# Talking-heads attention and a squared-ReLU feed-forward on one core: the score copies of a batch's last 64 tokens, one QK tile in batch 0, an earlier guard branch, and a new order of TensorE's work

## The chip, the cores and the metric

The kernel runs on one NeuronCore of a Trainium2 chip, as one program. The core has five engines that run side by side: TensorE (PE, matrix products; PEld is its weight load), VectorE (DVE), ScalarE (ACT), GpSimd (POOL) and SyncE (SP), and 16 DMA engines that all issue queues share. The metric is the device time of one execution in microseconds (us), the median of several. Matrix products write to PSUM, which has eight banks here; ACT or VectorE copy ("evict") each result to SBUF before its bank can be used again.

## The reference

Eight batches, twelve heads, 448 tokens, 64 channels per head; then a feed-forward over 8 x 448 = 3584 tokens of 768 channels.

```
scores = scale * q @ k.transpose(0, 1, 3, 2)
scores = einsum('bhij,hg->bgij', scores, w_pre)       # heads mixed before the softmax
attn   = exp(scores - max);  attn = attn / (sum(attn) + 1e-09)
attn   = einsum('bhij,hg->bgij', attn, w_post)        # heads mixed after the softmax
x      = (attn @ v), tokens x (heads * channels)
out    = (max(x @ w_in, 0) ** 2) @ w_out              # 768 -> 2048 -> 768
```

## The kernel before

**Stages of a batch.** Tokens are taken in chunks of ten (`CH`), 45 chunks per batch, the last one in two halves of four. A chunk holds 10 tokens x 12 heads = 120 rows, so that mixing the heads becomes a product with a 120-wide block matrix. A batch goes through these units on TensorE, each named in the code:

- `tr`: transposes of q and k (lines 833 and 837), copied to `qkt`.
- `qk`: scores of a tile of 128 tokens for one pair of heads (lines 975 and 985). The result, 128 tokens x 448 keys per head, is copied to `stage` (`sev`). The last tile of batches 1 to 7 has 64 tokens; there one unit does two pairs of heads, one in the upper and one in the lower 64 partitions of the bank, and each half is copied by itself: 64 partitions, twelve copies per batch.
- `rel`: a transfer on SP's queue that carries a chunk from `stage` (tokens in partitions) to `dring` (token and head in partitions); line 1030. `dring` has 16 slots, so a slot is written again when the pre unit 16 chunks earlier is done.
- `pre`: heads mixed before the softmax, two chunks at a time (lines 1054, 1061, 1069), followed by `exp` on ACT (line 1094), which also sums the rows.
- `rec` and `fold`: the reciprocal of the row sums and its product with the second mixing matrix, on POOL (lines 1117 and 1127; on VectorE for the first ten chunks).
- `post`: heads mixed after the softmax, transposed on the way (line 1159), copied to `a2t`.
- `av`: the product with v (lines 1216 and 1237), copied to `xt`.
- `h` and `o`: the two feed-forward products (lines 1288 and 1296; 1375, 1427 and 1435), with relu and square between them on ACT and VectorE; results go from `osb` to DRAM on SP's queue, the last ones on ACT's too.

In batch 0 the first 30 chunks (`ND`) don't go through `stage`: their scores are computed from a spread copy of q straight in dring's layout (`spr`, line 916). The remaining 148 tokens are two QK tiles (`NQ0`), each computed 128 tokens wide.

**Forms of a unit.** Many units can run as full 128-row products, as two row tiles of 64, or as four 64 x 64 quarters. The form is written into the order.

**What sets the order.** TensorE's order is the string `ORDER`: each character names the stream from which the next unit is taken and its form. A planner (`_Plan`) walks through it with a price for each task and places all other work: an eviction goes to whichever of ACT and VectorE would end it first by its prices, and the other engines' tasks are placed in the order in which they become ready. Every engine then executes its list in order, with semaphore waits. The price of `rec` on POOL is 120 ns (line 1123), while a `rel` is held at 1000 ns on SP.

**The guard.** The fast program takes the softmax without subtracting the maximum. VectorE checks the row sums once the last exp is done (`good0` to `good2`), SP turns the result into one row (`turn`), VectorE reduces it to one flag. At its end each engine waits for the flag, loads it (line 1631) and branches (line 1632): past a slow program with the maximum, in the normal case. SP's very last task, `final`, the waits for all outputs (line 1574), stands inside the branch.

Of the kernel before, what the change touches and what calls it, by code (L numbers as in the profile page):

```python
# [12 lines left out]
ACT = "act"  # L13
DVE = "dve"
POOL = "pool"
SP = "sp"
# [13 lines left out]
ORDER = (  # L30
    "0000511100551155555555555555555c2155555035bcb02515525353c2c5155c1531333355c2555c355332c0"
    "240443c4b200gh1111h62b3g33hqc31cgc3h2b3hgh3bbbch3633r3gb42444223g1h72qgqb2733g1r12q713h3"
    "6b2673722392003t122j33t2b282bi338333s04202444bb002gqbb28311i313s111s322gh2227hqh3613q1hr"
    "3363q2422444br2br631q1731h613q32h0220gh22qg373r3c38212i3s333814144420022ghh20028118111i1"
    "33s339b22j31t22193229119313t3319242444312q2bq227373163c3631731h2020q1g2br2h236333q20b0r2"
    "r20038318311i33184bb42244229c19311t133t118222833i313s242444232q2b623713733631g12r2br2006"
    "33q33rb17q200262r217293c3t331t2200jc181118133s311842244422391319313t13392422444222838333"
    "i311i31qb2b62qb2622h73733373q1b6rb00h2q0202q22h700239331911j11193182238318331s2424442228"
    "1s311i333814244413bq22g2rb2r23631q32r2br23633g31r002h2633q733r024044412tb2j0209bb2t23811"
    "381138333s11t22jb2922t23831s33i1318b4244422bq2bqb27337631q33731r2q21q2r22h1633673373bs22"  # L40
    "842i2i244422383833s333s22qr6r22293933t33tq4q444hghh6gq7g6hrghisrggh7hg7giqishhjjijtsttsj"
    "j"
)
# [329 lines left out]
def bass_talking_heads_attention__then__ffn_squared_relu_kernel(  # L373
# [17 lines left out]
    IT = 128  # L391
    ND = 30
    NE = 6
    NQ0 = 2
    QT0 = tuple((CH * (ND + x * (NCH - ND) // NQ0),
# [20 lines left out]
    with ExitStack() as es:  # L416
# [76 lines left out]
        def program(guard):  # L493
# [461 lines left out]
            def emit_QK(b, T):  # L955
# [7 lines left out]
                i0 = min(ta, S - w)  # L963
                for p in ((0, 3, 1, 4, 2, 5) if n == 0 else range(0, NP, IT // w)):
                    g = _Group(2)

                    quad = w == PJ
                    f = None if quad else _Flex(False)

                    def fn_qk(eng, en, p=p, g=g, f=f):  # L970
                        r_ = None
                        if f is not None and f.alt:
                            for x, y in QUADS:
                                r0 = 64 * x
                                r_ = eng.matmul(  # L975
                                    ps[y * PJ:(y + 1) * PJ, g.banks[x], 0:S],
                                    qkt[r0:r0 + 64, pb, p, 0, i0 + y * PJ:i0 + (y + 1) * PJ],
                                    qkt[r0:r0 + 64, pb, p, 1, :],
                                    start=True, stop=True,
                                )  # L980
                            return r_
                        for x, y in QUADS:
                            if y * w < IT:
                                r0 = 64 * x
                                r_ = eng.matmul(  # L985
                                    ps[y * w:(y + 1) * w, g.banks[x], 0:S],
                                    qkt[r0:r0 + 64, pb, p + y, 0, i0:i0 + w],
                                    qkt[r0:r0 + 64, pb, p + y, 1, :],
                                    start=True, stop=True,
                                )  # L990
                        return r_

                    t_qk = unit(s_QK, "qk%d_%d_%d" % (b, T, p), fn_qk,
                                [trev[(b, p + y)] for y in range(IT // w)]
                                + [trev.get((b, p + y, 0)) for y in range(IT // w)],
                                190.0, "quad" if quad else "row", g,
                                4 if quad else 2, f, [("quad", 190.0, 4)])
                    t_qk.after += old
                    for x, y in QUADS:
                        if y * w >= IT:  # L1000
                            continue

                        def fn_sev(eng, en, x=x, y=y, p=p, g=g):
                            return copy(eng, en, stage[0:w, sl, head(p + y, x), :],
                                        ps[w * y:w * y + w, g.banks[x], 0:S])

                        t_sev = add("sev%d_%d_%d_%d" % (b, T, p + y, x), FLEX, fn_sev, [t_qk] + old,
                                    c_ev(S), b * 1000.0 + 20 + 10 * T)
                        g.readers[x].append(t_sev)
                        sev_of[n].append(t_sev)  # L1010
# [3 lines left out]
                for c in range(NCP):  # L1014
                    i, nv = c * CH, CH
                    if c >= NCH - 1:
                        nv = TAIL // 2
                        i = S - TAIL + (c - NCH + 1) * nv
                    a, e = max(i, ta), min(i + nv, tb)
                    if a < e:  # L1020
                        emit_rel(b, c, n, a - i0, a - i, e - a)

            def emit_rel(b, c, n, r0, d0, nv):
                g = b * NCP + c
# [3 lines left out]
                def fn(eng, en):  # L1028
                    o = R0 + d0 * H
                    eng.dma_start(dring[o:o + nv * H, slot, :],  # L1030
                                  stage[r0:r0 + nv, n % 2, :, :]).then_inc(sem.handle, 16)

                t = plan.add("rel%d_%d_%d" % (b, c, d0), SP, fn, sev_of[n],
                             {SP: (1000.0, 0.0)}, g * 1.0, sem, 16,
                             dma=("move", 10.0 + 73.3 * nv, 54.0))
# [50 lines left out]
            def after_pre(g, t_pre, gr, x):  # L1086
# [28 lines left out]
                def fn_rec(eng, en):  # L1115
                    if en == POOL:
# [419 lines left out]
            if not guard:  # L1536
# [87 lines left out]
        def emit_engine(eng_name, eng):  # L1624
            tasks = fast[eng_name]
            k = len(tasks)
            while k and tasks[k - 1].name == "final":
                k -= 1
            emit_tasks(eng_name, eng, tasks[:k], fast_waits)
            eng.wait_ge(t_flag.sem.handle, t_flag.semval)  # L1630
            fine = eng.value_load(flag[0:1, 0:1])
            with eng.If(fine == 0):
# [56 lines left out]
```

## Time and profile before

| | |
|---|---|
| median of the runs | 533.03 us (531.01 to 534.14) |
| the profiled execution's own time | 531.75 us |
| its span, first to last instruction | 530.1 us |
| TensorE busy | 504.9 us, 95% |
| ACT busy | 429.9 us, 81% |
| VectorE busy | 387.7 us, 73% |
| POOL busy | 292.6 us, 55% |
| granted TensorE clock, mean | 0.996 |
| DMA moved | 71.10 MB, 134 GB/s mean |

The profile has one execution on the core. Its page lists busy time by engine, the chain of work that ended last, the costliest groups of instructions (line, engine, operation, out<-in, shapes, count, busy time and mean duration, and what ended the idle time before them) and the transfers. Views of the trace behind it give the waits by releaser, the busy time in stretches, and the instructions in order of time. A matmul's end is modelled, so that starts are the better measure for TensorE.

### The profile page before, as it was taken

Reading aid. Unit: us, or ns where it says so; the run is one execution under the profiler, and the core shown is the slowest. Engines: PE = TensorE matmul, PEld = TensorE weight load, DVE = VectorE, ACT = ScalarE, POOL = GpSimd, SP = SyncE. Lnnn points to the kernel's source line nnn. Section 1 sums busy time; section 2 is a strip of 40 time slices with the busy share of each in tenths; the row PEclk is TensorE's granted clock in tenths of the full one; section 3 lists DMA queues with packets and bytes.
Section 4 is the critical chain, followed back from the end, with each engine's and each line's share of the span. In section 5 each row is a group of like instructions: output and inputs, shape, how many; then the busy total and the mean of one; then the engine's idle time right before and its main releaser. Section 6 shows DMA issues by size and latency. Waiting matters only on the chain.

```text
span 530.1 us, 24988 instructions
## 1 busy us (share of the span) xinstructions
PE 504.9 (95%) x10519; PEld 329.4 (62%) x10519; DVE 387.7 (73%) x816; ACT 429.9 (81%) x1223; POOL 292.6 (55%) x524
## 2 busy tenths in 40 slices
PE   8999999999999999999899989999999999999994
PEld 4446776668765655666566655566666665678862
DVE  7898987889886699867787667776888668555400
ACT  5999989889978798888798878978978878977420
POOL 9847788527944597258752576416964445442000
PEclk9999999999999999999999999999999999999998
DMA  9999999646965799458954699536992567531022
GB/s 165 197 201 172 181 192 183 140 96 138 180 147 117 158 167 185 101 113 155 176 115 96 126 196 151 119 64 146 181 176 55 124 139 145 113 93 35 1 57 70
DMA packets 81811, 71.10 MB, mean 134 GB/s; under 512 B 13610, under 2 KB 78234, under 8 KB 81690
## 3 DMA queue, kind: packets, MB, share of 16 engines
q1 hardware_dynamic: 48138, 46.62, 36.1%
q0 software_dynamic: 33392, 22.59, 31.3%
q8 instruction: 86, 1.41, 1.1%
q14 instruction: 35, 0.29, 0.2%
q10 hardware_dynamic: 160, 0.20, 0.1%
HBM read 45.63 MB, written 11.01 MB: 107 GB/s over the span
## 4 chain that ended last, share of the span: by engine, by line
PE 72%; ACT 15%; POOL 7%; DVE 2%; issue 2%; DMA 1%; ACTq 0%; POOLq 0%
PE ps L1435 23%; PE ps L1296 13%; PE ps L1288 7%; PE ps L1159 7%; ACT pring L1094 6%; PE ps L1069 5%; PE ps L1237 5%; PE ps L985 4%; ACT stage L524 4%; POOL rinv L1117 3%; PE ps L1375 2%; PE ps L1427 2%; ACT dring L524 1%; POOL wk2s L1127 1%; PE ps L975 1%
## 5 line engine op out<-in xcount | busy, mean ns | idle before, releaser
L1117 POOL TENSOR_TENSOR rinv<-rowsum,minus 128x2 f32<-128x2 f32 (+1 forms) x179 | 126.1, 706 | 174.7 <-ACT pring L1094 173.9
L1094 ACT ACTIVATE pring<-ps 128x448 bf16<-128x448 f32 x360 | 192.3, 562 | 12.0 <-PE ps L1069 9.4
L525 DVE CAST a2t<-ps 128x480 bf16<-128x480 f32 (+1 forms) x205 | 124.8, 641 | 31.6 <-PE ps L1159 30.6
L1435 PE MATMUL ps<-w_out_sb,h2t 64*128 64x384 bf16 (+1 forms) x1728 | 141.4, 323 | 0.5 <-issue 0.4
L525 DVE CAST stage<-ps 128x448 bf16<-128x448 f32 (+1 forms) x193 | 115.0, 617 | 25.8 <-PE ps L985 15.1
L1296 PE MATMUL ps<-xt,w_in_sb 64*64 64x448 bf16 (+4 forms) x1872 | 121.0, 327 | 1.8 <-issue 1.2
L524 ACT ACTIVATE a2t<-ps 128x480 bf16<-128x480 f32 (+1 forms) x163 | 87.6, 581 | 22.5 <-PE ps L1159 21.7
L1435 PEld LDWEIGHTS ps<-w_out_sb,h2t 64*128 64x128 bf16 (+1 forms) x1728 | 74.6, 97 | 45.1 <-issue 1.9
L524 ACT ACTIVATE stage<-ps 128x448 bf16<-128x448 f32 (+1 forms) x167 | 87.0, 549 | 14.3 <-PE ps L985 9.6
L1296 PEld LDWEIGHTS ps<-xt,w_in_sb 64*64 64x64 bf16 (+1 forms) x1872 | 65.0, 102 | 34.5 <-issue 2.5
L1094 ACT ACTIVATION_READ_ACCUMULATOR pring<-ps 128x1 f32 x360 | 81.6, 227 | 0.0
L1127 POOL TENSOR_TENSOR wk2s<-wk2b,rinv 128x120 bf16<-128x120 bf16 (+1 forms) x179 | 70.7, 396 | 12.4
L1159 PEld LDWEIGHTS ps<-wk2s,pring 60*128 60x128 bf16 x2880 | 56.6, 93 | 31.9 <-DVE a2t L525 4.8
L1159 PE MATMUL ps<-wk2s,pring 60*128 60x60 bf16 x2880 | 64.8, 187 | 6.9 <-POOL wk2s L1127 4.2
L1343 DVE TENSOR_TENSOR h2t<-h1t 128x448 bf16<-128x448 bf16 (+2 forms) x176 | 53.3, 331 | 23.3 <-ACT h1t L1333 22.5
L1069 PE MATMUL ps<-dring,wk 64*64 64x448 bf16 (+1 forms) x622 | 54.5, 359 | 2.6 <-ACT h1t L1333 0.9
L1333 ACT ACTIVATE h1t<-ps 128x448 bf16<-128x448 f32 (+2 forms) x93 | 40.4, 439 | 14.4 <-PE ps L1288 5.9
L1334 DVE TENSOR_SCALAR h1t<-ps 128x448 bf16<-128x448 f32 (+2 forms) x83 | 41.3, 505 | 11.4 <-PE ps L1296 8.4
L1288 PE MATMUL ps<-xt,w_in_sb 128*128 128x220 bf16 (+2 forms) x420 | 47.4, 265 | 0.2
L1288 PEld LDWEIGHTS ps<-xt,w_in_sb 128*128 128x128 bf16 x420 | 38.2, 98 | 7.3 <-ACT pring L1094 0.9
L985 PE MATMUL ps<-qkt 64*128 64x448 bf16 (+1 forms) x288 | 39.5, 353 | 1.4 <-DVE a2t L525 0.8
L738 POOL DMA_DIRECT2D vraw<-in_v_dram x54 | 34.3, 640 | 0.0
(76 smaller groups left out, 434.2 us busy)
## 6 DMA issues: line engine op xcount, KB each, us to landing
dring<-stage SPq DMA_DIRECT2D x301, 105.0 KB
out_dram<-osb SPq DMA_DIRECT2D x45, 192.0 KB, 3.6
qraw<-in_q_dram POOLq DMA_DIRECT2D x42, 112.0 KB, 5.0
kraw<-in_k_dram POOLq DMA_DIRECT2D x42, 112.0 KB, 5.1
w_in_sb<-in_moe_w_in_dram POOLq DMA_DIRECT2D x8, 384.0 KB, 10.2
w_out_sb<-in_moe_w_out_dram POOLq DMA_DIRECT2D x8, 384.0 KB, 8.9
vraw<-in_v_dram POOLq DMA_DIRECT2D x21, 128.0 KB
vraw<-in_v_dram POOLq DMA_DIRECT2D x21, 96.0 KB
```

The source lines that it names most:

```text
L524: return eng.activation(o, i_, AF.Copy)
L525: return eng.tensor_copy(o, i_)
L985: r_ = eng.matmul(ps[y * w:(y + 1) * w, g.banks[x], 0:S], qkt[r0:r0 + 64, pb, p + y, 0, i0:i0 + w], qkt[r0:r0 + 64, pb, p + y, 1, :], star ...
L1069: r_ = eng.matmul(ps[64 * y:64 * y + 64, gr.banks[x], 0:S], wk1[64 * x:64 * x + 64 - R0 * x, 64:128], dring[64 * x:64 * x + 64 - R0 * x, ( ...
L1094: return eng.activation(pring[:, pr, 0:S], ps[:, gr.banks[x], 0:S], AF.Exp, accum_out=rowsum[:, g, :])
L1117: return eng.tensor_tensor(rinv[:, p0:p0 + n, :], rowsum[:, g0:g0 + n, :], minus1[:, 0:n, :], ALU.pow)
L1127: return eng.tensor_tensor(wk2s[:, p0:p0 + n, :], i0.to_broadcast([128, n, PR]), rinv[:, p0:p0 + n, :].to_broadcast([128, n, PR]), ALU.mult)
L1159: r_ = eng.matmul(ps[:, gr.banks[x], o0:o0 + PR], pring[64 * x:64 * x + PR, pr + y, j0:j0 + 2 * PJ], wk2s[64 * x:64 * x + PR, pr + y, :], ...
L1288: r_ = eng.matmul(ps[:, g.banks[ph], 0:n], w_in_sb[:, ft, t * 128:(t + 1) * 128], xt[:, ft, c0:c1], start=(ft == 0), stop=(ft == NFT - 1))
L1296: r_ = eng.matmul(ps[z:z + w, g.banks[x], 0:n], w_in_sb[64 * y:64 * y + 64, ft, t * 128 + z:t * 128 + z + w], xt[64 * y:64 * y + 64, ft, c ...
L1343: return eng.tensor_tensor(h2t[:, t16, o0:o0 + n], h1t[:, s, 0:n], h1t[:, s, 0:n], ALU.mult)
L1435: r_ = eng.matmul(ps[z:z + w, g.banks[hh], 0:FH], h2t[64 * y:64 * y + 64, t16, col + z:col + z + w], w_out_sb[64 * y:64 * y + 64, t16, hh ...
```

## The change

Five things change.

- **Tail scores.** For the 64-token tile of batches 1 to 7, a unit now takes the pairs p and p + 3 instead of p and p + 1, and each bank is copied to `stage` in one instruction of 128 partitions: partitions 0 to 63 hold the even heads and 64 to 127 the odd ones. Six copies per batch take the place of twelve. The transfer of such a chunk becomes two, one for the even and one for the odd heads, each to every second row of `dring`; the planner's price for it on SP stays 1000 ns.
- **Batch 0.** `ND` goes from 30 to 32 and `NQ0` from 2 to 1: 320 tokens by the direct way, and the other 128 in one QK tile.
- **Guard branch.** Two marker tasks, `turnact` and `turnsp`, split the lists of ACT and SP: what comes behind the marker is emitted inside both sides of the branch, so that these two engines load the flag and branch before their last work (in the planned order ACT after the fifth relu of batch 7, SP after the output copies of batch 6's tile 1). PE, VectorE and POOL branch at their ends, as before.
- **Price.** `rec` on POOL is 700 ns instead of 120 in the planner.
- **Order.** `ORDER` is a new string. Against the old one, 54 copies to `stage` and six QK units fall away, two `spr` chunks with a copy each are added, the forms of some pre and feed-forward units differ, and nearly every unit stands in another place.

```
-    ND = 30
+    ND = 32
     NE = 6
-    NQ0 = 2
+    NQ0 = 1
...
+                            if quad:
+                                r_ = eng.matmul(
+                                    ps[y * w:(y + 1) * w, g.banks[x], 0:S],
+                                    qkt[r0:r0 + 64, pb, p + 3 * y, 0, i0:i0 + w],
+                                    qkt[r0:r0 + 64, pb, p + 3 * y, 1, :],
+                                    start=True, stop=True,
+                                )
...
-                        def fn_sev(eng, en, x=x, y=y, p=p, g=g):
-                            return copy(eng, en, stage[0:w, sl, head(p + y, x), :],
-                                        ps[w * y:w * y + w, g.banks[x], 0:S])
+                    for x in range(2):
+                        h = 2 * p + x if quad else head(p, x)
+
+                        def fn_sev(eng, en, x=x, h=h, g=g):
+                            return copy(eng, en, stage[:, sl, h, :], ps[:, g.banks[x], 0:S])
...
-                    eng.dma_start(dring[o:o + nv * H, slot, :],
-                                  stage[r0:r0 + nv, n % 2, :, :]).then_inc(sem.handle, 16)
+                    for y in range(2 if two else 0):
+                        i_ = stage[64 * y + r0:64 * y + r0 + nv, n % 2, 0:H // 2, :]
+                        eng.dma_start(dring[o + y:o + nv * H:2, slot, :], i_).then_inc(sem.handle, 16)
+                    if not two:
+                        eng.dma_start(dring[o:o + nv * H, slot, :],
+                                      stage[r0:r0 + nv, n % 2, :, :]).then_inc(sem.handle, 16)
...
-                            {DVE: (82.0, 160.0), POOL: (120.0, 180.0)}, b * 1000.0 - 900 + c)
+                            {DVE: (82.0, 160.0), POOL: (700.0, 750.0)}, b * 1000.0 - 900 + c)
...
+                for en in (ACT, SP):
+                    plan.add("turn" + en, en, None, [t_flag], {en: (3600.0, 3600.0)}, -1e8)
...
-            while k and tasks[k - 1].name == "final":
-                k -= 1
+            for i, t in enumerate(tasks):
+                if t.name == "turn" + eng_name:
+                    k = i
+            rest = tasks[k + 1:]
             emit_tasks(eng_name, eng, tasks[:k], fast_waits)
             eng.wait_ge(t_flag.sem.handle, t_flag.semval)
             fine = eng.value_load(flag[0:1, 0:1])
             with eng.If(fine == 0):
-                emit_tasks(eng_name, eng, tasks[k:], fast_waits)
+                emit_tasks(eng_name, eng, rest, fast_waits)
                 for s_, v_ in reached:
                     eng.wait_ge(s_.handle, v_)
                 emit_tasks(eng_name, eng, slow[eng_name], slow_waits)
-            if k < len(tasks):
+            if rest:
                 with eng.Else():
-                    emit_tasks(eng_name, eng, tasks[k:], fast_waits)
+                    emit_tasks(eng_name, eng, rest, fast_waits)
```

More of the change, by code (lines that the diff above doesn't have):

```diff
@@ L963, in emit_QK @@
                 i0 = min(ta, S - w)
-                for p in ((0, 3, 1, 4, 2, 5) if n == 0 else range(0, NP, IT // w)):
+                for p in ((0, 3, 1, 4, 2, 5) if n == 0 else range(NP * w // IT)):
                     g = _Group(2)
@@ L971, in fn_qk @@
                         r_ = None
-                        if f is not None and f.alt:
-                            for x, y in QUADS:
-                                r0 = 64 * x
+                        for x, y in QUADS:
+                            r0 = 64 * x
+                            if quad:
[5 more added lines that the diff above has]
+                                )
+                            elif f.alt:
                                 r_ = eng.matmul(
@@ L980, in fn_qk @@
                                 )
[L981 to L984, printed above, removed]
+                            elif y == 0:
                                 r_ = eng.matmul(
-                                    ps[y * w:(y + 1) * w, g.banks[x], 0:S],
-                                    qkt[r0:r0 + 64, pb, p + y, 0, i0:i0 + w],
-                                    qkt[r0:r0 + 64, pb, p + y, 1, :],
+                                    ps[0:w, g.banks[x], 0:S],
+                                    qkt[r0:r0 + 64, pb, p, 0, i0:i0 + w],
+                                    qkt[r0:r0 + 64, pb, p, 1, :],
                                     start=True, stop=True,
@@ L993, in emit_QK @@
                     t_qk = unit(s_QK, "qk%d_%d_%d" % (b, T, p), fn_qk,
-                                [trev[(b, p + y)] for y in range(IT // w)]
-                                + [trev.get((b, p + y, 0)) for y in range(IT // w)],
+                                [trev[(b, q_)] for q_ in ((p, p + 3) if quad else (p,))]
+                                + [trev.get((b, p, 0))],
                                 190.0, "quad" if quad else "row", g,
@@ L1020, in emit_QK, with emit_rel @@
                     if a < e:
-                        emit_rel(b, c, n, a - i0, a - i, e - a)
-            def emit_rel(b, c, n, r0, d0, nv):
+                        emit_rel(b, c, n, a - i0, a - i, e - a, w == PJ)
+            def emit_rel(b, c, n, r0, d0, nv, two):
                 g = b * NCP + c
```

30 lines of the change are left out of this document (13 added, 17 removed).

## The prediction

> **What bounds the kernel now.** I read the page's head first, then the busy time by stage, then who TensorE waited for, and last the end of the trace.
>
> ```profile
> span 530.1 us, 24988 instructions
> PE 504.9 (95%) x10519; PEld 329.4 (62%) x10519; DVE 387.7 (73%) x816; ACT 429.9 (81%) x1223; POOL 292.6 (55%) x524
> PE 72%; ACT 15%; POOL 7%; DVE 2%; issue 2%; DMA 1%; ACTq 0%; POOLq 0%
> ```
>
> TensorE is busy for 504.9 of 530.1 us and carries 72% of the chain that ended last, so 25.2 us of idle time is most of what a change that leaves its work alone can win. Where that idle time lies, by stage:
>
> ```profile
> 484.00:522.00 38.00, 38.00 (x339) 29.46 (x332) 9.37 (x34) 13.52 (x35) 0.00 (x0) 1.00 0.17 42
> 522.00:530.00 8.00, 0.36 (x3) 0.00 (x0) 0.00 (x0) 0.49 (x1) 0.00 (x0) 0.74 0.26 66
> ```
>
> These are the last two of eleven stretches; the columns are the stretch, its length, and busy time of PE, PEld, DVE, ACT and POOL. The last 8 us hold 0.36 us of TensorE work: 7.6 us of tail. Of the rest, these are the waits of TensorE:
>
> ```profile
> PE ps L1159 <- POOL wk2s L1127: 4.2, 5, 1.3
> PE ps L661 <- DVE warm L646: 1.4, 1, 1.4
> ...
> PE ps L916 <- ACT a2t L524: 0.2, 1, 0.2
> ```
>
> There are 22 such rows from the first to the last shown. By releaser they add up to 4.2 us for POOL's folding of the reciprocals, 6.2 us for ACT and VectorE (14 rows of 0.2 to 0.9), 3.5 us for "issue" (6 rows) and 1.4 us for the warm-up's operand. No row names a transfer: the score copies into dring arrive in time.
>
> **The change part by part.**
>
> *Scores of the last 64 tokens.* Before, each of batches 1 to 7 copies twelve blocks of 64 partitions out of PSUM; after, six of 128.
>
> ```profile
> L525 DVE CAST stage<-ps 128x448 bf16<-128x448 f32 x148 | 87.5, 617 | 21.9 <-PE ps L985 12.2 <-PE ps L975 8.0 <-issue 0.8
> L524 ACT ACTIVATE stage<-ps 128x448 bf16<-128x448 f32 x128 | 66.4, 553 | 12.0 <-PE ps L985 7.9 <-PE ps L975 2.6 <-DMA dring<-stage 1.1
> L525 DVE CAST stage<-ps 64x448 bf16<-64x448 f32 x45 | 27.5, 620 | 3.8 <-PE ps L985 3.0
> L524 ACT ACTIVATE stage<-ps 64x448 bf16<-64x448 f32 x39 | 20.6, 537 | 2.3 <-PE ps L985 1.7
> ```
>
> The 64-row copies cost what the 128-row ones cost (620 against 617 ns, 537 against 553), so halving their number halves 27.5 + 20.6 = 48.1 us: 24 us less on the two engines together. Batch 0 loses one of two QK tiles, 12 copies, and gains two directly multiplied chunks with a copy each: another 10 x 0.58 = 6 us. In all 30 us of 817.6 (3.7%). None of it is on the path as such, since neither engine is the bound. What it can win is a share of TensorE's 6.2 us of waits for them. I take 2.5 us: more than in proportion, because a wait is the excess of a queue over its lead. Ends: 0, and all 6.2.
>
> *TensorE's own work.* Rows of starts give the prices.
>
> ```profile
> 25.63 0.55 PE L1054 MATMUL ps<-dring,wkf 128*128 128x448 bf16 x2
> 26.11 0.56 PE L916 MATMUL ps<-qkt,h2t 128*32 128x448 bf16 x8
> 26.61 0.40 PE L1159 MATMUL ps<-wk2s,pring 60*128 60x60 bf16 x16
> 26.93 0.56 PE L916 MATMUL ps<-qkt,h2t 128*32 128x448 bf16 x8
> ...
> 146.58 0.38 PE L1069 MATMUL ps<-dring,wk 64*64 64x448 bf16 x4
> 146.79 0.36 PE L985 MATMUL ps<-qkt 64*64 64x448 bf16 x4
> ...
> 216.41 0.40 PE L1159 MATMUL ps<-wk2s,pring 60*128 60x60 bf16 x16
> 216.64 0.37 PE L985 MATMUL ps<-qkt 64*128 64x448 bf16 x2
> 216.83 1.48 PE L1435 MATMUL ps<-w_out_sb,h2t 64*128 64x384 bf16 x16
> ```
>
> From start to start, a QK unit takes 0.19 us (216.64 to 216.83), a quartered pre unit 0.21 (146.58 to 146.79). A post unit takes 0.23 where the same tiling follows (216.41) and 0.32 where another does (26.61), so a change of tiling costs 0.09. A full pre unit takes 0.48 with a change, 0.39 without, and a directly multiplied chunk 0.41 (0.50 less the change). Counted over both program orders: six QK units less (-1.1), two chunks more (+0.8), one pair of batch 0 from quartered to full (+0.2), six more pre units in two row passes instead of four quarters (6 x 0.18 = +1.1), ten more changes of tiling (+0.9). Sum +1.9 us, on the path in full, since TensorE has little idle time to hide it in. The feed-forward units that change form count as nothing: the same columns stream. The ends are +0.5, if half of the changes fall into waits, and +3.
>
> *POOL's reciprocal at 700 ns, not 120, in the planner, and the new order.* No instruction changes, only where each stands.
>
> ```profile
> L1117 POOL TENSOR_TENSOR rinv<-rowsum,minus 128x2 f32<-128x2 f32 (+1 forms) x179 | 126.1, 706 | 174.7 <-ACT pring L1094 173.9
> ...
> 306.74 0.71 POOL L1117 TENSOR_TENSOR rinv<-rowsum,minus 128x2 f32<-128x2 f32 x1
> 307.41 0.67 POOL L699 DMA_DIRECT2D kraw<-in_k_dram  x1
> 308.10 0.40 POOL L1127 TENSOR_TENSOR wk2s<-wk2b,rinv 128x120 bf16<-128x120 bf16 x1
> 308.64 0.40 PE L1159 MATMUL ps<-wk2s,pring 60*128 60x60 bf16 x16 [1.31 <-POOL wk2s L1127]
> ```
>
> The reciprocal takes 706 ns. In the longest of the five waits POOL runs it, issues a load that the old price placed there, and folds only then; TensorE stands for 1.31 us. With the true price the load moves and posts are placed later: in the old order eleven posts have under 3.5 us of TensorE work (by the prices above) between their pre and themselves, the least 2.6; in the new one five, the least 3.0. I let 3.2 of the 4.2 us go. The ends are 0 and 4.2. What would be late next is the ACT queue, which feeds POOL, and that has lost 29 copies. The "issue" waits (3.5 us) stay: nothing in the diff prices them otherwise, and where a wait of that kind falls moves with every order.
>
> *The guard branch ahead of results.* ACT and SP test the flag now before their last output work; the other engines test it as before.
>
> ```profile
> L1631 ACTq TENSOR_LOAD <-flag x1: 1121/1121/1121, 523.4 to 523.4; - x1
> ...
> L1632 POOLq COMPARE_BRANCH  x1: 45/45/45, 485.4 to 485.4; - x1
> ...
> L1632 PEldq COMPARE_BRANCH  x1: 3721/3721/3721, 519.9 to 519.9; - x1
> ...
> L1632 SPq COMPARE_BRANCH  x1: 50/50/50, 525.1 to 525.1; - x1
> L1574 SPq EVENT_SEMAPHORE  x2: 17/22/28, 528.3 to 528.4; - x2
> L1641 POOLq DRAIN  x1: 3567/3567/3567, 488.4 to 488.4; - x1
> L1641 ACTq DRAIN  x1: 81/81/81, 527.9 to 527.9; - x1
> ...
> L1641 SPq EVENT_SEMAPHORE  x1: 17/17/17, 528.8 to 528.8; - x1
> ...
> L1641 ACTq EVENT_SEMAPHORE  x1: 17/17/17, 530.0 to 530.0; - x1
> ...
> 520.82 3.19 SPq L1398 DMA_DIRECT2D out_dram<-osb  x3
> ...
> out_dram<-osb SPq DMA_DIRECT2D x20, 96.0 KB, 2.5
> ```
>
> POOL, which has nothing left to wait for, goes 3.0 us without an instruction after its branch (485.4 to 488.4); SP goes 3.2 (525.1 to 528.3). The last output's issue ends at 524.0, so began about 0.6 earlier, and lands 2.5 us after that, at 525.9; SP looks at 528.3 only. Without the flag test there SP goes on at 525.9 and the closing barrier, 0.5 us (528.3 to 528.8), ends at 526.4, against 530.05. That is 3.7 us at best. If ACT's last step still comes 1.2 us after the others (530.0 against 528.8) it is 2.4. I take 3.1. TensorE's own branch ends at 519.9 + 3.7 = 523.6 and doesn't bind. In exchange ACT stands for 4.5 us after the flag (its load at 523.4 to its next instruction at 527.9), in a stage where it works 13.5 of 38 us, and VectorE, at 9.4 of 38, gets five of its copies in the new order. SP stands 4 us, with output copies behind it that nothing reads for some 20 us. I charge 0.5 us; the ends are 0 and 4.5, the whole stand.
>
> On the price of a branch the Trainium skill, "Advanced Engine Details and Errata", section Control Flow Timing, gives about 108 ns for a compare-and-branch. The trace agrees for the instruction (45 to 72 ns on four engines) and not for the 3 us behind it; by that figure the tail would gain 0.1 us, and the sum would be 3 us higher.
>
> *Two transfers where one was.* The rows of the last 64 tokens go out as even and odd heads: 16 issues per batch, not 8, on SP's queue.
>
> ```profile
> L1030 SPq DMA_DIRECT2D dring<-stage x359: 667/825/2033, 29.3 to 465.4; - x180
> ...
> 111.98 6.47 SPq L1030 DMA_DIRECT2D dring<-stage  x7
> ...
> 117.57 0.76 PE L1069 MATMUL ps<-dring,wk 64*64 64x448 bf16 x10
> ```
>
> Smaller issues should cost between the least, 667 ns, and the median, 825. At 0.75 a batch's tail takes 16 x 0.75 - 8 x 0.825 = 5.4 us longer on SP. I cost it at nothing, because the cover is the lead of the ring: dring holds 16 chunks, and no wait of TensorE names a transfer. The shortest lead I see is at batch 2's first pair: two of seven issues are out at 113.8, and TensorE reads them at about 117.8, 4 us later. If that cover is gone, the cost is up to 5.4 us in each of seven batches.
>
> *Sum*, against the profiled execution's 531.75 us (its span and 1.65 around it): -2.5 + 1.9 - 3.2 - 3.1 + 0.5 = -6.4, so 525.35. That execution lies 1.3 us under the median of the runs shown, 533.03, and I add a quarter of it: **525.7 us**. Between 531.0 and 534.1 of those runs, 0.5% (2.7 us) is about what can be told from no change.
>
> **The rivals.**
>
> *A, the sum above*: 521.5 to 529, 525.7. Chance 0.52.
>
> *B, only the tail is won.* The waits fall elsewhere in the new order, as each order has its own. The many waits of 0.2 to 0.9 us speak for it; the looser posts speak against it. 531.75 + 1.9 + 0.5 - 3.1 = 531. Chance 0.15, half of it inside 0.5%.
>
> *C, SP's queue becomes the bound, slower.* Place: the last three pairs of each batch and the first of the next, behind 16 issues. With 5.4 us more against the 4 us lead above, 1.4 us is late in a batch like the second; it decides once the leads of most batches are as short as that one and a landing takes its part of them. Say 1.4 us issue and 1 to 2 us landing in four batches, 10 to 14 us: 525.4 + 12 = 537. Against it: SP stood idle between the tail of one batch and the head of the next (it was on its output issues and then waited up to 111.98). Chance 0.11.
>
> *D, the waits mostly go.* With POOL's and both evicting engines' waits gone but 1 us (9.4), the tail at 3.7, and some of the issue waits: 531.75 + 1.9 - 9.4 - 3.7 - 1.5 = 519. Chance 0.17.
>
> *E, the branch doesn't do what it says.* The idle 3 us after it aren't the branch's, or ACT's and SP's early ones starve TensorE by 4.5 us. No tail gain in the first form: 525.35 + 3.1 = 528.4. Against it stands POOL's row, where nothing else can hold the engine. Chance 0.05. The Trainium skill's figure above would be this rival's first form.
>
> **How the numbers follow.** The prediction is A's, 525.7. The range from 518 to 532 takes in D and most of B and E, leaves out C and the tails: 0.8. Under 530.4 (faster by over 0.5%) lie A but for 0.02, D, half of B and most of E: 0.50 + 0.17 + 0.07 + 0.04 = 0.78. Over 535.7 lies C but for 0.01: 0.10. The rest, 0.12, is within 0.5%.
>
> **What would show each step.** The stage copies of 64 rows gone from the groups, and their 128-row groups with 54 fewer in all than 360. The wait row of L1159 on POOL's wk2s at about 1 us. TensorE's last matmul some 3 us earlier (519), and from it to the end of the span 4 to 5 us where it was 7.7; ACT's and SP's flag loads near 480, not 524. SP's dring issues up by 54 with a median near 0.8, and still no wait on dring's transfers. A row in which TensorE waits for dring, or an ACT gap of over 5 us near 485 with TensorE idle beside it, would make the prediction wrong, and so would a sum of "issue" and eviction waits that hasn't fallen.

## The result: slower, and the profile after

The median of 20 runs after the change is 539.05 us (530.96 to 544.64), against 532.0 us (529.8 to 538.28) in 20 runs of the kernel before. The ratio of the runs is 1.0077, with a 95% interval of 1.0048 to 1.0106; it leaves out every run more than 1.5% above the fastest of its kernel, and since the changed kernel's runs spread evenly over 14 us, 11 of its 20 fall out. Over all runs the medians stand 1.013 apart. Either way the change loses where 525.7 us was forecast, and the median lies outside the range (518 to 532).

The page of the profiled execution of the changed kernel (537.8 us, span 536.0), its head, the TensorE clock in 40 slices, and the chain that ended last by engine:

```profile
span 536.0 us, 24801 instructions
PE 508.0 (95%) x10441; PEld 332.8 (62%) x10441; DVE 379.9 (71%) x806; ACT 412.3 (77%) x1181; POOL 290.8 (54%) x524
PEclk9989999999999999999999999999989999998999
PE 76%; DMA 7%; ACT 5%; DVE 4%; SPq 3%; issue 3%; POOL 0%; DVEq 0%; POOLq 0%
```

ACT and VectorE have lost work (429.9 to 412.3 and 387.7 to 379.9 us, together 25 of the forecast 30), and the kernel is slower all the same. New in the chain are DMA at 7%, where it was 1%, and SP's queue at 3%, where it had no share. TensorE's last matmul now ends at 530.98, not 522.36: 8.6 us later. Of these, 3.1 us are busy time (508.0 against 504.9) and 5.5 us standstill (23.0 against 17.5 ahead of the last matmul). The stretch behind it shrank, from 7.7 to 5.0 us. The loss is thus inside the pipeline.

TensorE's waits in the changed kernel, the longest first (line, releaser, us in total, times, longest; "issue" is a standstill for which the view names no engine and no transfer):

```profile
PE ps L1074 <- DMA dring<-stage: 3.4, 4, 1.6
PE ps L1074 <- DVE osb L524: 3.1, 2, 2.2
PE ps L974 <- issue: 2.8, 2, 2.6
PE ps L1164 <- issue: 2.6, 2, 1.8
...
PE ps L1074 <- DVE h2t L1348: 1.4, 1, 1.4
```

L1074 is the pre unit on two row passes, the reader of `dring`. The five rows of that line which name an engine or a transfer add up to 9.5 us; the same unit's add up to 1.7 us before. The first row is the one the prediction called its refutation. POOL's 4.2 us on wk2s are gone from the list.

The transfers also hold the evictions. ACT and VectorE copy scores into `stage`, which has two buffers, and must wait until the transfers have read the older tile:

```profile
ACT stage L523 <- DMA dring<-stage: 4.0, 5, 1.8
```

```profile
DVE stage L524 <- DMA dring<-stage: 4.2, 5, 1.6
```

Those were 1.1 and 0.5 us before, once each. Now SP's own issues, grouped by line (duration of one in ns: least, median, longest; first and last start). L1033 is the doubled transfer, L1035 the single one:

```profile
L1033 SPq DMA_DIRECT2D dring<-stage x112: 643/769/1632, 98.5 to 475.9; - x112
L1035 SPq DMA_DIRECT2D dring<-stage x301: 672/853/2256, 30.6 to 460.3; - x151
```

A transfer of half as many rows takes SP 769 ns at the median, against 853 for the others: half the rows cost nine tenths of an issue. In order of time on SP's queue in batch 3, where one tail ends and the next tile starts:

```profile
275.64 3.43 SPq L1478 DMA_DIRECT2D out_dram<-osb  x3
279.12 13.15 SPq L1033 DMA_DIRECT2D dring<-stage  x16
292.37 1.88 SPq L1478 DMA_DIRECT2D out_dram<-osb  x2
294.35 11.71 SPq L1035 DMA_DIRECT2D dring<-stage  x12
```

From 275.6 to 306.1 SP issues without a gap of more than 0.1 us. At the same place before, its queue was not full:

```profile
274.40 7.19 SPq L1030 DMA_DIRECT2D dring<-stage  x8
282.43 1.18 SPq L1473 DMA_DIRECT2D out_dram<-osb  x2
286.41 14.19 SPq L1030 DMA_DIRECT2D dring<-stage  x15
```

Behind the eight issues of the tail it stood idle for 0.8 us, and behind the two output rows for 2.8 us: 3.6 us in all. What TensorE sees of the full queue in the changed kernel, in order of time; the last column is the idle time and what ended it:

```profile
296.90 0.57 PE L1074 MATMUL ps<-dring,wk 64*64 64x448 bf16 x6
299.05 0.38 PE L1074 MATMUL ps<-dring,wk 64*64 64x448 bf16 x4 [1.58 <-DMA dring<-stage]
```

The row "DVE osb" leads to the same queue by a longer way. Near the last tail SP issued sixteen half-size transfers from 463.9 to 476.5, and only then an output row, whose two copies to `osb` had ended at 469.2 (from 469.7 on the view shows the last nine of the sixteen):

```profile
468.62 0.49 ACT L523 ACTIVATE osb<-ps 128x384 f32<-128x384 f32 x1 [0.16 <-PE ps L1440]
468.62 0.56 DVE L524 COPY osb<-ps 128x384 f32<-128x384 f32 x1 [4.72 <-PE ps L1440]
...
469.70 6.84 SPq L1033 DMA_DIRECT2D dring<-stage  x9
476.65 5.61 SPq L1478 DMA_DIRECT2D out_dram<-osb  x4
```

The chain that ended last goes on from that issue. (It puts the step ahead of it down to VectorE's copies to `a2t`, which the output doesn't read.)

```profile
476.76 0.43 SPq L1478
...
477.24 3.29 DMA out_dram<-osb
480.56 0.57 DVE osb L524
481.18 0.38 PE ps L1074 x4
```

The output row's issue stands behind the tail's for 7.5 us; it lands late, `osb` comes free late, VectorE empties the PSUM bank late, and the pre unit, which needs that bank, starts 2.16 us late. An output that nothing downstream reads still sets when a buffer and a bank come free.

A standstill of such a length can cost twice. Busy time in stretches (the stretch, its length, busy PE, PEld, DVE, ACT, POOL, granted clock, DMA share, GB/s):

```profile
35.00:39.00 4.00, 4.00 (x42) 0.95 (x36) 1.97 (x4) 2.81 (x9) 0.35 (x1) 0.57 0.85 161
...
397.00:401.00 4.00, 4.00 (x60) 2.06 (x58) 1.53 (x4) 0.77 (x2) 0.00 (x0) 0.57 0.57 130
...
478.00:482.00 4.00, 1.84 (x72) 1.42 (x64) 0.56 (x1) 1.44 (x6) 0.00 (x0) 1.00 0.40 89
482.00:486.00 4.00, 3.97 (x53) 2.17 (x46) 1.06 (x3) 2.20 (x10) 3.15 (x6) 0.57 0.40 102
490.00:498.00 8.00, 8.00 (x156) 6.82 (x149) 6.32 (x19) 2.35 (x6) 0.00 (x0) 1.00 0.23 56
531.00:536.00 5.00, 0.00 (x0) 0.00 (x0) 0.00 (x0) 0.49 (x1) 0.00 (x0) 0.76 0.34 88
```

After standing 2.65 us (393.6 to 396.2) and 2.16 us (479.0 to 481.2), TensorE runs 4 us at a mean granted clock of 0.57; 0.43 of 4 us is 1.7 us lost each time. A third such stretch, 35 to 39 us, follows a standstill of 1.77 us. Only the standstill at 479 goes back to SP's queue, the other two are "issue" waits. The kernel before has no such stretch ahead of its last matmul.

### The profile page after: what moved, and what is told of

It is laid out like the page before. It is cut to its first block, busy times and chain, and to the rows that moved or that the text cites. A ratio compares the mean times of both kernels' runs of the same rounds, so it can differ in the third digit from the quotient of the medians.

```text
span 536.0 us, 24801 instructions
## 1 busy us (share of the span) xinstructions
PE 508.0 (95%) x10441; PEld 332.8 (62%) x10441; DVE 379.9 (71%) x806; ACT 412.3 (77%) x1181; POOL 290.8 (54%) x524
## 4 chain that ended last, share of the span: by engine, by line
PE 76%; DMA 7%; ACT 5%; DVE 4%; SPq 3%; issue 3%; POOL 0%; DVEq 0%; POOLq 0%
PE ps L1440 20%; PE ps L1301 17%; PE ps L1293 9%; PE ps L1164 6%; PE ps L1074 6%; DMA dring<-stage 5%; PE ps L1242 5%; SPq L1033 3%; ACT pring L1099 3%; PE ps L988 3%; PE ps L1380 2%; PE ps L1432 2%; PE ps L915 2%; DVE stage L524 2%; PE ps L836 2%
## 5 line engine op out<-in xcount | busy, mean ns | idle before, releaser
L524 DVE CAST a2t<-ps 128x480 bf16<-128x480 f32 (+1 forms) x209 | 126.6, 641 | 37.6 <-PE ps L1164 36.7
L524 DVE CAST stage<-ps 128x448 bf16<-128x448 f32 x168 | 99.9, 618 | 31.1 <-PE ps L981 11.4
L1301 PE MATMUL ps<-xt,w_in_sb 64*64 64x448 bf16 (+4 forms) x1728 | 109.5, 329 | 0.1
L523 ACT ACTIVATE stage<-ps 128x448 bf16<-128x448 f32 x138 | 72.2, 556 | 18.7 <-PE ps L988 6.5
L1301 PEld LDWEIGHTS ps<-xt,w_in_sb 64*64 64x64 bf16 (+1 forms) x1728 | 60.4, 103 | 29.8 <-issue 2.3
L1132 POOL TENSOR_TENSOR wk2s<-wk2b,rinv 128x120 bf16<-128x120 bf16 (+1 forms) x179 | 69.0, 388 | 10.2
L1074 PE MATMUL ps<-dring,wk 64*64 64x448 bf16 (+1 forms) x592 | 53.0, 360 | 10.0 <-DMA dring<-stage 3.4
L1293 PE MATMUL ps<-xt,w_in_sb 128*128 128x220 bf16 (+2 forms) x480 | 59.1, 276 | 0.0
L1293 PEld LDWEIGHTS ps<-xt,w_in_sb 128*128 128x128 bf16 x480 | 43.8, 98 | 12.3 <-issue 2.8
L523 ACT ACTIVATE osb<-ps 128x384 f32<-128x384 f32 x31 | 15.1, 492 | 27.2 <-PE ps L1432 8.6
L1242 PE MATMUL ps<-a2t,vraw 128*64 128x228 bf16 (+1 forms) x640 | 35.2, 261 | 0.0
## 6 DMA issues: line engine op xcount, KB each, us to landing
qraw<-in_q_dram POOLq DMA_DIRECT2D x42, 112.0 KB, 5.1
kraw<-in_k_dram POOLq DMA_DIRECT2D x42, 112.0 KB, 5.1
```

The costliest lines, as they stand in the source:

```text
L523: return eng.activation(o, i_, AF.Copy)
L524: return eng.tensor_copy(o, i_)
L1074: r_ = eng.matmul(ps[64 * y:64 * y + 64, gr.banks[x], 0:S], wk1[64 * x:64 * x + 64 - R0 * x, 64:128], dring[64 * x:64 * x + 64 - R0 * x, ( ...
L1132: return eng.tensor_tensor(wk2s[:, p0:p0 + n, :], i0.to_broadcast([128, n, PR]), rinv[:, p0:p0 + n, :].to_broadcast([128, n, PR]), ALU.mult)
L1242: r_ = eng.matmul(ps[kk * 64:kk * 64 + 64, g.banks[x_], x * n:(x + 1) * n], vraw[:, h, s, :], a2t[half][:, s, h, a0:a0 + n], start=(rest a ...
L1293: r_ = eng.matmul(ps[:, g.banks[ph], 0:n], w_in_sb[:, ft, t * 128:(t + 1) * 128], xt[:, ft, c0:c1], start=(ft == 0), stop=(ft == NFT - 1))
```

## The experiments

Times are medians; the ratio is to the kernel before, run beside it on the same chip with a median of 531.1 to 531.4.

**The changed kernel with a single transfer.** The tail goes back to the pairs p and p + 1, twelve copies of 64 rows and one transfer; order, batch 0, price and branch stay as changed.

```
-                for p in ((0, 3, 1, 4, 2, 5) if n == 0 else range(NP * w // IT)):
+                for p in ((0, 3, 1, 4, 2, 5) if n == 0 else range(0, NP, IT // w)):
...
-                            return copy(eng, en, stage[:, sl, h, :], ps[:, g.banks[x], 0:S])
+                            return copy(eng, en, stage[0:w, sl, head(p + y, x), :],
+                                        ps[w * y:w * y + w, g.banks[x], 0:S])
...
-                        emit_rel(b, c, n, a - i0, a - i, e - a, w == PJ)
+                        emit_rel(b, c, n, a - i0, a - i, e - a, False)
```

> The changed kernel with the copies of the last 64 tokens as before (twelve of 64 rows, one transfer per chunk); its order string, batch 0, prices and early branch stay. Theory Q (the doubled transfers fill SP's queue, the ring's lead is used up and TensorE stands for dring): the waits for dring go, the lead returns, and the time falls to 530 to 533 us although 24 us of copies come back. Theory O (the new order has waits of its own, fetches above all): the time stays at 536 to 540. If the saved copies were worth something: above 540.

526.52 us (521.4 to 528.3), ratio 0.988 [0.983, 0.993], which is less than any of the times expected. It was measured a second time, unchanged:

> The kernel with single transfers unchanged, once more beside its two variants: 525 to 528, and faster than the kernel before by 0.8 to 1.5%.

525.64 us (523.9 to 529.6), ratio 0.989 [0.984, 0.994]: the best version of all, ahead of both kernels. None of the 12 runs of the two is as long as the changed kernel's fastest. The second one's page, its waits on `stage` and its SP queue at the corresponding tail:

```profile
span 524.2 us, 24801 instructions
PE 504.6 (96%) x10441; PEld 331.6 (63%) x10441; DVE 392.9 (75%) x827; ACT 421.6 (80%) x1202; POOL 289.9 (55%) x524
PE 83%; ACT 6%; DVE 6%; issue 2%; DMA 1%; POOL 0%; POOLq 0%; ACTq 0%; DVEq 0%
```

```profile
ACT stage L523 <- DMA dring<-stage: 0.3, 1, 0.3
```

```profile
270.29 3.39 SPq L1477 DMA_DIRECT2D out_dram<-osb  x3
274.53 7.21 SPq L1034 DMA_DIRECT2D dring<-stage  x8
281.84 1.65 SPq L1477 DMA_DIRECT2D out_dram<-osb  x2
283.59 12.42 SPq L1034 DMA_DIRECT2D dring<-stage  x13
```

Eight issues in 7.2 us stand where sixteen in 13.15 us stood: 5.9 us per tail, close to the 5.4 of the prediction. With them gone, SP's queue leaves the chain, no row of TensorE names a transfer of dring, the waits of the same pre unit but for "issue" fall from 9.5 to 1.0 us, and TensorE's last matmul ends at 519.1, 11.9 us before the changed kernel's. ACT and VectorE have more to do than in the changed kernel (421.6 and 392.9 us) and it is faster all the same. The copies saved and the transfers doubled are one edit here; whether a single transfer could take rows from both halves of `stage` wasn't tried.

**The kernel before with the doubled transfer alone.** Copies, pairs and order stay as they were; each tail chunk goes out as even and odd heads.

```
-                    eng.dma_start(dring[o:o + nv * H, slot, :],
-                                  stage[r0:r0 + nv, n % 2, :, :]).then_inc(sem.handle, 16)
+                    for y in range(2 if two else 0):
+                        i_ = stage[r0:r0 + nv, n % 2, y:H:2, :]
+                        eng.dma_start(dring[o + y:o + nv * H:2, slot, :], i_).then_inc(sem.handle, 16)
...
-                             {SP: (1000.0, 0.0)}, g * 1.0, sem, 16,
+                             {SP: (1000.0, 0.0)}, g * 1.0, sem, 32 if two else 16,
```

> The kernel before with one thing added: the transfer of each chunk of the last 64 tokens is issued as two, even and odd heads; copies, order and all else stay. Theory Q: 4 to 8 us slower than before (536 to 540), waits of pre units for dring appear. Theory O: within 1 us of before, since the old order's lead of 4 us and more covers 5.4 us of issue per batch.

546.69 us, ratio 1.030 [1.026, 1.035]: 15.3 us, twice the most that was expected and the largest price of any part. Waits of ACT and VectorE for `stage`, and TensorE's first wait:

```profile
ACT stage L524 <- DMA dring<-stage: 10.4, 8, 3.0
```

```profile
DVE stage L525 <- DMA dring<-stage: 12.6, 6, 2.8
```

```profile
PE ps L1073 <- DVE stage L525: 5.2, 4, 2.8
```

The two engines together wait 23 us, mostly at the same moments, where they waited 1.6 us. The buffer that runs out is `stage`, and TensorE then waits on the copies more than on the transfers (0.3 us on those of `dring`).

**The kernel before with the two-head copies and the doubled transfer**, in the old order.

```
-                for p in ((0, 3, 1, 4, 2, 5) if n == 0 else range(0, NP, IT // w)):
+                for p in ((0, 3, 1, 4, 2, 5) if n == 0 else range(NP * w // IT)):
...
-                            return copy(eng, en, stage[0:w, sl, head(p + y, x), :],
-                                        ps[w * y:w * y + w, g.banks[x], 0:S])
+                            return copy(eng, en, stage[:, sl, h, :], ps[:, g.banks[x], 0:S])
...
-                        emit_rel(b, c, n, a - i0, a - i, e - a)
+                        emit_rel(b, c, n, a - i0, a - i, e - a, w == PJ)
```

> The kernel before with the two-head copies whole: six copies of 128 rows and two transfers per chunk, old order string, old price, old branch, old batch 0. Theory Q: as the one with the doubled transfers alone, less at most 2.5 us for the saved copies: 534 to 539. Theory O: 529 to 532, the copies' gain without a cost.

540.09 us, ratio 1.015 [1.011, 1.019]. Against the run above, the six copies saved per batch are worth 6.6 us where SP holds up the evictions (the pairs and the source rows of the transfers change with them); they pay back less than half of what their transfers cost.

**Queue time or transfers.** To the kernel before, eight issues of 4 bytes each per batch are added on SP, one behind every tail chunk; the copies are read by nothing. The transfers that matter stay whole.

```
+                    if two:
+                        i = 2 * dummies["n"]
+                        dummies["n"] += 1
+                        eng.dma_start(spare[0:1, i:i + 2], ident[0:1, 0:2]).then_inc(sem_spare, 16)
```

> The kernel before with eight issues more per batch on SP, one behind each chunk of the last 64 tokens, that carry only 4 bytes from a constant to a spare place: SP's queue is charged as by the doubled transfers and the score transfers stay whole. Theory Q, the queue's time alone: 8 to 15 us slower (540 to 546), as with the doubled transfers (546.7). If two half transfers were the harm (more descriptors in flight, landing later): within 2 us of before, 530 to 533.

541.9 us, ratio 1.020 [1.015, 1.024]: 10.6 us. SP's issues of it, and the evictions' waits:

```profile
L1038 SPq DMA_DIRECT2D spare<-ident x56: 610/617/659, 102.3 to 480.7; - x56
```

```profile
DVE stage L528 <- DMA dring<-stage: 10.9, 6, 3.2
```

The issues move 224 bytes in all, and take 4.9 us of SP's queue per batch (8 x 0.617). They bring back the waits and two thirds of the doubled transfer's loss. Queue time alone is thus enough for that much. The doubled transfer adds 5.7 us per batch (16 x 0.769 less 8 x 0.825); in proportion the 10.6 us would be 12.3. The last 3 us of 15.3 are hardly more than the two intervals leave open (2.5 us each way); they may be the nonlinear end of a queue that runs over, or something in the half transfers.

**Output rows issued by POOL**, in the changed kernel and in the one with a single transfer, to take 2.2 to 3.4 us at a time off SP.

```
-                    o_free[s].append(plan.add("odma%d_%d_%d" % (b, tile, x), SP, fn_od, evs,
-                                              {SP: (720.0, 0.0)}, b * 1000.0 + 710, sem_out[s], 16,
+                    o_free[s].append(plan.add("odma%d_%d_%d" % (b, tile, x), POOL, fn_od, evs,
+                                              {POOL: (720.0, 0.0)}, b * 1000.0 + 710, sem_out[s], 16,
```

> The changed kernel with the 59 issues of finished output rows moved from SP to POOL; the doubled transfers stay. If it is the time of SP's queue that was short (theory Q), some 40 us of issue leave it, the waits for dring go and the time falls to 526 to 531 us. If the doubled transfers hurt by themselves (landing later, holding DMA engines) or the order does, it stays at 535 to 540.

> The changed kernel with single transfers and 64-row copies, which ran at 526.5, and the output issues moved to POOL as well. Theory Q, with SP short only beyond its load in the kernel before: no further gain, 525 to 527. If SP was already short there: 521 to 524. If POOL's issues delay its folds: above 528.

535.58 us, ratio 1.006 [1.002, 1.010] with doubled transfers (12 runs, one of which took 1739.7 us), and 533.64, ratio 1.004 [1.001, 1.007] with single ones. In the second POOL's part does 7 to 8 us of harm by itself, against 526.5 and 525.6 us. TensorE's first wait of each, in that order:

```profile
PE ps L1164 <- POOL wk2s L1132: 5.5, 6, 2.2
```

```profile
PE ps L1163 <- POOL wk2s L1131: 4.7, 5, 2.2
```

and POOL's own, in the first: an output issue stands in its queue until the evictions that it sends have been made (the row names what ACT, which makes them, ended last), and the folding of reciprocals stands behind it.

```profile
POOL out_dram L1478 <- ACT pring L1099: 21.2, 7, 5.2
```

With outputs off SP, doubling the transfers costs 1.9 us (535.58 against 533.64), which the two intervals don't tell from nothing; with outputs on SP, 12.5 to 13.4 by the medians. That doesn't show that the sixteen issues are free there. In the first, evictions still wait 14.8 us for the transfers, against 1.7 in the second:

```profile
ACT stage L523 <- DMA dring<-stage: 6.6, 4, 3.0
...
DVE stage L524 <- DMA dring<-stage: 8.2, 6, 2.9
```

In both TensorE waits longest for POOL, and the price of the doubled transfers may be hidden behind that. What it would be with the outputs off SP and POOL free wasn't tried.

**Odd heads issued by ACT**, in the changed kernel, on a semaphore of their own; the even ones stay on SP.

```
+                    t = plan.add("rem%d_%d_%d" % (b, c, d0), ACT, fn2, sev_of[n],
+                                 {ACT: (530.0, 0.0)}, g * 1.0, sem2, 16,
+                                 dma=("move", (10.0 + 73.3 * nv) / 2, 54.0))
```

> The changed kernel with the second of the two transfers (odd heads) issued by ACT instead of SP, on a semaphore of its own. Theory Q: SP's load falls below that of the kernel before, the dring waits go; ACT gains 56 issues of 0.53 us, 30 us, as much as the copies saved on both engines, and a wait in ACT's queue can stand before evictions: 526 to 532. If the number of transfers hurts and not the queue: 535 to 540.

568.49 us, ratio 1.068 [1.064, 1.073], more than any of the times expected. An issue takes ACT 0.79 us at the median, not the planned 0.53. The eight of a tail mostly go out one behind another, in 6.3 to 9.9 us, with exponentials behind them, and TensorE waits for those. The longest such case on ACT, and TensorE's first wait:

```profile
348.99 9.09 ACTq L1051 DMA_DIRECT2D dring<-stage  x7
358.12 0.54 ACT L1114 ACTIVATE pring<-ps 128x448 bf16<-128x448 f32 x1 [9.54 <-issue]
```

```profile
PE ps L1089 <- ACT pring L1114: 17.1, 4, 8.2
```

SP is relieved and the kernel takes 30 us more than the changed one, so free time on an engine says nothing of what a row of issues holds up in its queue.

**The branch alone**, on the kernel before, and **the branch put back** to the end of ACT's and SP's work in the version with a single transfer. The first adds these lines, the second takes them away:

```
+                for en in (ACT, SP):
+                    plan.add("turn" + en, en, None, [t_flag], {en: (3600.0, 3600.0)}, -1e8)
...
-            while k and tasks[k - 1].name == "final":
-                k -= 1
+            for i, t in enumerate(tasks):
+                if t.name == "turn" + eng_name:
+                    k = i
+            rest = tasks[k + 1:]
```

> The kernel before with the early branch of ACT and SP alone. Both theories: the tail after TensorE's last matmul is 5.0 us as in the changed kernel, not 7.7, and the time falls by 2 to 3 us to about 529.5. If ACT's early stand starves TensorE there, no gain, and a gap of TensorE near 487.

> The same with single transfers (526.5 us) and the guard branch at the end of all engines as in the kernel before. The tail is 7.7 us again instead of about 4.8, so 529 to 530. If the early branch is worth nothing: 526 to 527.

The first takes 529.99 us, ratio 0.997 [0.994, 1.000], some 1.4 us less than before with an interval that reaches no change; from TensorE's end to the span's end it has 4.6 us where before has 7.7, but TensorE's end is 2.1 us later, by waits elsewhere. The second takes 528.06, ratio 0.994 [0.991, 0.997], 2.4 us more than the 525.64 measured beside it; its stretch behind TensorE is 6.3 us long, not the expected 7.7, against 5.1. So the branch is worth 1.4 to 2.4 us by the medians, and neither figure is clear of its interval.

**The price alone**, on the kernel before, and **the old price** in the version with a single transfer.

```
-                            {DVE: (82.0, 160.0), POOL: (120.0, 180.0)}, b * 1000.0 - 900 + c)
+                            {DVE: (82.0, 160.0), POOL: (700.0, 750.0)}, b * 1000.0 - 900 + c)
```

> The kernel before with the planner's price of 700 ns for the reciprocal on POOL alone, under the old order string. If the price by itself moves POOL's loads out from between reciprocal and fold: TensorE's waits for wk2s fall from 4.2 to about 1 us and the time to 528 to 530. If the posts' places in the order string are what matters: no difference, 531 to 533, the waits stay.

> The new order, batch 0 and branch with single transfers (526.5 us) and the old price of 120 ns. If the price carries the gone waits on POOL: waits for wk2s are back at 4 us and the time is 530 to 532. If the places of the posts in the new order carry them: 525 to 528.

533.06 us, ratio 1.000 [0.997, 1.003], and 526.83, ratio 0.988 [0.983, 0.994]. The price does nothing that can be measured in either. With the true price and the old order, TensorE's wait for POOL is still there (in an execution of 537.8 us):

```profile
PE ps L1159 <- POOL wk2s L1127: 6.1, 3, 4.3
```

With the old price and the new order it is 1.6 us, and with the true price and the new order there is no row. What took most of these waits away is where the posts stand in the new order.

## Why the prediction was wrong

**Two transfers where one was: the step that failed.** "I cost it at nothing, because the cover is the lead of the ring." The size of the edit was right (5.4 us per batch; 5.9 in the timelines), the cover was not. The lead of the ring was looked at chunk by chunk and found 4 us at its shortest, but the 5.4 us of one tail fall on everything in SP's queue behind it: the next tile's chunks, the output rows, and through these `stage`'s second buffer, `osb` and a PSUM bank. "No wait of TensorE names a transfer" was true of before and said nothing of how near the queue was to full: its 359 chunk issues at 825 ns alone are 296 us of it, each in order, many behind waits that nothing can use. The row that warned of it was there, and read as nothing: `stage` evictions already waited twice for transfers, 1.6 us. In the changed kernel the doubling costs 12.5 to 13.4 us by the medians (539.05 against 526.52 and 525.64) and some 10 us by the ratios, net of the copies saved.

**Rival C was what happened.** Its place (the last pairs of a batch and the first of the next, behind sixteen issues) is where the timeline shows SP full. That its 537 us lie 2 us under the median is partly luck: its sum counts chunks that come late to the ring, and the runs show the loss going through `stage` and `osb` as well. Its argument against itself, that SP stood idle between tail and head, was right for before, but there was too little of it: 2.3 us in the batch it looked at (from the last output row, 109.7, to 112.0) and 3.6 us in batch 3, less than the 5.4 us that were to go in. The chance of 0.11 should have been weighed by that comparison.

**The rest of the sum held as a total.** Without the doubled transfer the change gives 525.6 and 526.5 us where the sum said 525.7. That is luck in good part, since that version keeps the twelve copies whose saving the sum counted, and the parts miss in both directions:

- *The branch, -3.1 + 0.5.* The tail behind the last matmul went from 7.7 to 5.0 us: 2.7 won. The charge for ACT standing was too much: from 490 to 498 us, around ACT's flag load at 493.1 (near 480 was forecast), TensorE is busy all 8.00 us. As a whole 1.4 to 2.4 us, near the forecast 2.6.
- *POOL's waits, -3.2.* They went entirely, by 4.2 us, but for the most part by the order and not by the price.
- *The copies, -2.5.* Six per batch fell away and ACT and VectorE waited more, since transfers held them. In the version with single transfers, which keeps the twelve copies, TensorE's waits for ACT and VectorE, without the warm-up's, are 4.8 us against 6.2: 1.4 of the 2.5 came, but with the order (and batch 0, which was not run apart from it). That fewer copies win anything where SP isn't late was not shown; where it is late they win 6.6 us.
- *TensorE's own work, +1.9.* In the version with single transfers TensorE is busy for 504.6 us, 0.3 less than before, and that includes a stretch at a lower clock. The rise in the changed kernel (3.1 us) goes with its three such stretches, 1.7 us each. Without them, both come to an estimated 502.9 us, 2.0 less than before: the +1.9 isn't seen, and its sign looks wrong. Which of its counts or prices is at fault wasn't tested.
- *The "issue" waits* "stay", it said. They rose from 3.5 to 7.8 us in the changed kernel and to 7.2 with single transfers, and took back about what POOL's waits gave. They come with the new order, and the traces say more of them than the view does. The page of each profile lists a queue that carries instructions:

```profile
q8 instruction: 86, 1.41, 1.1%
```

All 52 "issue" waits of 0.6 us or more, over the fourteen profiles, end 1.3 to 1.6 us after one of these 86 transfers of 16 KB has ended. That fits TensorE standing there for its own instructions, though no run changed anything about it. Why these waits are longer in the new order stays open.

The time of the single-transfer version can be read from its trace: against before, TensorE's last matmul ends 3.3 us earlier (519.1 against 522.36), where the sum without the tail's 3.1 us said 3.3; by the bullets above, the two agree by parts that cancel.

## What to carry to other kernels

A queue that issues in order has a load like an engine, and size makes little difference to an issue (0.62 us here for 4 bytes, some 0.85 us for 105 KB): before splitting a transfer, sum up the issues per period and look for the idle stretches that are to take the new ones, at the tightest place. A buffer's lead towards its reader is only one side; the other is the release of the buffer it is read from, and a small wait of the evictions on a transfer says that this side has run out already. Moving issues to a less busy engine is no way out if they stand there ahead of work that others need.

## What the runs showed that had not been expected

TensorE's clock fell to half after short standstills: in the changed kernel 1.8 to 2.65 us of idle time were followed by 3.4 us at half speed, 1.7 us lost each (at 35, 397 and 482 us), though 1.58 us at 297 was not. The length alone doesn't decide it: with the two-head copies in the old order a standstill of 2.51 us was not followed by a slower stretch, while one of 1.4 us was in the single-transfer version with outputs on POOL. The clock goes with the spread of the changed kernel's times: at 530.96 us the mean clock is 0.997, at 543.6 to 544.6 us it is 0.978 to 0.982, which makes an estimated 8 to 10 of the 13 us between them. Why the clock differs from run to run wasn't settled. And 4-byte transfers, eight per batch, that nobody waits for, cost 10.6 us.
